# A state-space kernel with two heads: transposing loads for x, B, C, k and v, B's factor moved to C, and a shift convolution by channels

## The chip, the cores and the metric

The kernel runs on one core of a Trainium2 chip. The metric is device time in microseconds (us), the median of several timed runs; lower is better. The engines are TensorE (PE in the profile, its weight loads PEld), VectorE (DVE), ScalarE (ACT), GpSimd (POOL) and SyncE (SP), which here issues nearly all DMAs. SBUF holds one tile, the *arena*; PSUM holds one tile, *acc*, with eight banks of 512 f32 columns.

## The reference

Two heads on sequences of 2,048 steps with 640 channels, their outputs side by side in `[2048, 1280]`, inputs and output bf16:

```python
# head A: a diagonal state space with 640 complex states
dt = exp(log_dt);  Lam = Lambda_re + 1j * Lambda_im
Lam_bar = exp(dt * Lam)
B_bar = ((Lam_bar - 1.0) / Lam)[:, None] * (B_re + 1j * B_im)
Bu = einsum("bld,pd->blp", x, B_bar)
h_t = Lam_bar * h_(t-1) + Bu_t                        # 2048 steps
y = 2.0 * einsum("blp,dp->bld", h, C_re + 1j * C_im).real + x * Dskip

# head B: a short and a long convolution with gates
k_shift[s] = sum(k[s - j] * shift_k[:, j] for j in 0..3)   # zeros before the start
kv = k_shift * v
y = irfft(rfft(kv padded to 4096) * rfft(ssm_k padded to 4096))[:2048]
y = q * (y + kv * ssm_D)

out = concatenate([a, b], -1)
```

## The kernel before

**How it is ordered.** Each step is an operation of `Program.add`: a name, the engines that may do it, what it reads and writes in the arena, and a PSUM group. `depend()` derives the dependences from the footprints. The string `ORDER` (L1034), lists every operation as number, engine letter (T, V, A, G for POOL, S for SP) and first PSUM bank; `emit` issues the operations in that order, each engine's own in its order of the list, with semaphore waits for the dependences between engines. What shares a buffer or a bank waits for its last user.

**Tables.** `setup` makes the DFT tables. W (for the second transform step) is made in four chunks: an iota on POOL, two ACT operations `w_q` (L286) that multiply by the row number, a mask on DVE `w_a` (L289), and a sine on ACT (L292). G (for the last inverse step) has four chunks too: iota (L317) and integer product `g_q` (L320) on POOL, a sine on ACT (L322), two masked copies `g_k` (L325). `params` (L330) turns Lambda and dt into powers of the decay: `spread` (L420) makes 128x1280 diagonal blocks, once as GM (the factor of B) and four times as RR (the decay of the tree); DG (L427) is Dskip on diagonals; L437 to L442 make the sine and cosine of the scan's phase, the product at L440 on POOL.

**Head A.** The 640 states are ten blocks j of 64, real and imaginary part stacked on 128 partitions. B is loaded in rows (L466), and `prep_B` (L511) multiplies it by GM on TensorE (L522), which turns it at once; eviction at L528. x comes in sixteen loads of 128 rows (L474, steps of 16 in time, bit-reversed order) and is turned by TensorE in pairs (`turn_x`, L503, eviction L508). The recurrence is a tree over 16 neighbouring steps: `up2`, `up1`, `up0` (L538 to L596) take the base products B·x (`base`, L533, five of 128x512) and add the lower levels with the decay (`rmm`, L552); `coarse` (L602) scans over the 128 groups of 16 on DVE with a rotation by the phase; `down` (L638) goes back: products with the decay (L655), then either an addition on DVE (L673), or an identity product on TensorE (L653) with a copy on ACT (L671). `load_C` (L480) writes C's two planes into DRAM in the blocks' order, and one transposing DMA (L489) reads them back into the buffer that held B. `project` (L677) makes one output block of 128 rows: twenty products with C (L687, two halves of 320 columns), six with DG for x·D (L692), one copy on ACT (L696), a store (L699).

**Head B.** The long convolution of length 4,096 is a DFT in two steps of 64, in two halves (hf) of 320 channels. k is loaded with rows of 64 steps as columns (L755), its halo in small loads (L759), v alike (L768). `conv` (L780) forms the shift convolution on 2,560 elements a partition: four products with a spread table SK (`tap`, L795), three additions (L800), a product with v (L801), for each of two column sets per half; two of the 32 operations run on POOL, the rest on DVE. `s1` (L803) is the first step: ten groups of 32 products (L820) in quarters of the array, for the filter h and for k; k's stationary operands have a step of 40 elements. Evictions at L825 go to the buffer AS. `s2` (L828) is the second step: 24 products (or 16) of 160 columns in two column halves per group (L838), evicted at L851, for h into Y and for k into AS. `product` (L854) is the complex product, four times per half: pp (L862, 2,560 elements), two pq (L865), py (L867) and pz (L869), all on DVE. `r2` (L883, eviction L888) and `r1` (L904) go back; r1's eviction (L916) multiplies by q, and `store` (L928) writes. Both halves use the same AS, Y, kt, vt.

**The order of the work.** Tables, parameters and turns; up; down; in between the filter's s1 and s2 of half 0; then k's s1, the middle and the way back of half 0, half 1 alike, the sixteen projections spread over the second half and the end. `load_C` runs between up and projections.

Of the kernel before, what the change touches and what calls it, by code (L numbers as in the profile page):

```python
# [9 lines left out]
ALU = mybir.AluOpType  # L10
# [172 lines left out]
for _name, _n in (("A", 10 * 16 * 130), ("BT", 6400), ("RR", 5120), ("W", 4096), ("G", 8192), ("XT", 10240), ("AS", 10240),  # L183
                  ("Y", 10240), ("T", 7680), ("H0", 5120), ("K0", 5504), ("V0", 5120), ("YS", 2560), ("SN", 1024), ("I3", 192), ("E", 64),
                  ("JS", 128), ("F1", 128), ("IDF", 192), ("DG", 640), ("SK", 640), ("DM", 160),
                  ("PV", 70), ("SMALL", 1400)):
    LAY.part(_name, _n)


class Ctx:  # L190
    def __init__(self, nc, tc, arena, psum, ins, out):
        self.nc, self.arena = nc, arena
        self.P = Program(nc, arena, psum)
        self.ins, self.out = ins, out.rearrange("b s d -> (b s) d")
        self.CP = {nc.scalar: nc.scalar.copy, nc.vector: nc.vector.tensor_copy, nc.gpsimd: nc.gpsimd.tensor_copy}
        self.small_at = LAY.at["SMALL"][0]
# [19 lines left out]
def setup(c):  # L216
# [13 lines left out]
    P.add("js0", {V: .2}, lambda e: e.tensor_scalar_mul(out=JS[:, 0:64], in0=I3[:, 64:128], scalar1=-1.0), outs=[JS[:, 0:64]],  # L230
          ins=[I3[:, 64:128]])
    P.add("js1", {V: .2}, lambda e: e.tensor_copy(out=JS[:, 64:128], in_=I3[:, 128:192]), outs=[JS[:, 64:128]],
# [24 lines left out]
    scr = c.arena[:, LAY.at["A"][0]:LAY.at["A"][0] + 20800]  # L257
    m1 = scr[:, 20000:20064].bitcast(i32)
    q1 = scr[:, 20064:20192].bitcast(i32)
    s1 = scr[:, 20192:20320].bitcast(f32)  # L260
# [12 lines left out]
    offw = f(2)  # L273
    for lo, b, val in ((0, 0, 6144.0), (0, 1, 8192.0), (64, 0, 4096.0), (64, 1, 6144.0)):
        P.add("offw", {V: .1}, lambda e, lo=lo, b=b, val=val: e.memset(offw[lo:lo + 64, b:b + 1], val),
              outs=[offw[lo:lo + 64, b:b + 1]])
    mw = scr[:, 0:4096].bitcast(i32)
    qw = scr[:, 4096:12288].bitcast(i32)
    for ch in range(4):
        mc = mw[:, 512 * ch:512 * ch + 512]  # L280
        qc = qw[:, 1024 * ch:1024 * ch + 1024]
        q4 = qc.rearrange("p (k b c) -> p k b c", k=8, b=2)
        P.add("w_m", {G: .6}, lambda e, mc=mc, ch=ch: e.iota(mc, pattern=[[4, 8], [128, 64]], base=1 + 32 * ch,
                                                               channel_multiplier=0), outs=[mc])
        for b in range(2):
            P.add("w_q", {A: .8}, lambda e, q4=q4, mc=mc, b=b: e.activation(  # L286
                out=q4[:, :, b, :], in_=mc.rearrange("p (k c) -> p k c", k=8), func=FN.Identity, scale=p63, bias=offw[:, b:b + 1]),
                outs=[q4[:, :, b, :]], ins=[mc, p63, offw])
        P.add("w_a", {V: .7}, lambda e, qc=qc: e.tensor_single_scalar(out=qc, in_=qc, scalar=8191, op=ALU.bitwise_and),  # L289
              outs=[qc], ins=[qc])  # L290
        wo = Wt[:, 8 * ch:8 * ch + 8, :].rearrange("p k c -> p (k c)")
        P.add("w_s", {A: 1.15}, lambda e, qc=qc, wo=wo: e.activation(out=wo, in_=qc, func=FN.Sin, bias=npi, scale=SC13),  # L292
              outs=[wo], ins=[qc, npi])

    IDF = c.IDF = v("IDF")
    mi = scr[:, 20320:20448].bitcast(i32)
    qi = scr[:, 19000:19384].bitcast(i32)
# [6 lines left out]
    P.add("i_s", {A: .38}, lambda e: e.activation(out=IDF, in_=qi, func=FN.Sin, bias=npi, scale=SC13), outs=[IDF], ins=[qi, npi])  # L304

    Gt = c.G = v("G").rearrange("p (r b e a) -> p r b e a", r=2, b=64, e=2)
# [5 lines left out]
    sn = v("SN")  # L312
    for ch in range(4):
        ri, bh = ch // 2, ch % 2
# [7 lines left out]
        P.add("g_s", {A: 1.07}, lambda e, qc=qc: e.activation(out=sn, in_=qc, func=FN.Sin, scale=SC), outs=[sn], ins=[full])  # L322
        for el in range(2):
            go = Gt[:, ri, 32 * bh:32 * bh + 32, el, :]
            P.add("g_k", {V: .47, G: 2.9}, lambda e, go=go, el=el: e.tensor_scalar(  # L325
                out=go, in0=sn.rearrange("p (b a) -> p b a", a=32), scalar1=mk[:, el:el + 1], scalar2=None, op0=ALU.mult),
# [3 lines left out]
def params(c):  # L330
# [5 lines left out]
    tk = f(4)  # L336
    P.add("pr0", {V: .15}, lambda e: e.memset(pr, 0.0), outs=[pr])
    for k, src in enumerate((lam_re, lam_im, ldt_in)):
        rows = pr[10 * k:10 * k + 10, :]
        P.add("ld_par", {PSP: .1, A: .1}, lambda e, rows=rows, src=src: e.dma_start(  # L340
            out=rows.rearrange("p (a b) -> p a b", a=2), in_=bass.AP(src.tensor, 0, [[64, 10], [0, 2], [1, 64]])),
            outs=[tk[:, k:k + 1]], ins=[pr], nbytes=2560)
    rows5 = pr[30:35, :]
    P.add("ld_par", {PSP: .1, A: .1}, lambda e: e.dma_start(out=rows5, in_=dsk_in.rearrange("(a b) -> a b", b=128)),
          outs=[tk[:, 3:4]], ins=[pr], nbytes=1280)
    PV = v("PV").bitcast(f32)
    g = P.group(1)
    P.add("t_par", {PPE: .1}, lambda e, B: e.matmul(B[:, 0:35], lhsT=pr, rhs=c.I3[:, 0:35], start=True, stop=True), ins=[tk, c.I3[:, 0:35]],
          group=g, nmm=1)
    P.add("pv", {V: .25}, lambda e, B: e.tensor_copy(out=PV, in_=B[:, 0:35]), outs=[PV], group=g)  # L350
    lre, lim, ldt, dsk = PV[:, 0:10], PV[:, 10:20], PV[:, 20:30], PV[:, 30:35]
# [21 lines left out]
    for lo, mi, val in ((0, 0, 2 ** 30), (0, 1, -2 ** 31), (64, 0, 0), (64, 1, 2 ** 30)):  # L373
# [18 lines left out]
    dc, sg = f(2), f(1)  # L392
    for lo, mi, val in ((0, 0, 1.0), (0, 1, 0.0), (64, 0, 0.0), (64, 1, 1.0)):
        P.add("dc", {V: .1}, lambda e, lo=lo, mi=mi, val=val: e.memset(dc[lo:lo + 64, mi:mi + 1], val), outs=[dc[lo:lo + 64, mi:mi + 1]])
    for lo, val in ((0, 2.0), (64, -2.0)):
        P.add("sg", {V: .1}, lambda e, lo=lo, val=val: e.memset(sg[lo:lo + 64, :], val), outs=[sg[lo:lo + 64, :]])
# [56 lines left out]
class PartA:  # L453
# [57 lines left out]
    def prep_B(self, u):  # L511
# [15 lines left out]
        def ev(e, B):  # L527
            c.CP[e](out=out, in_=B[:, 0:n])  # L528
# [611 lines left out]
```

## Time and profile before

| | us |
|---|---|
| timed runs | 231.92 (median), 230.56, 231.97 |
| profiled execution | 229.08 |
| its span | 227.3 |

A busy time is the sum of an engine's instructions; idle time inside the span is a wait. How the busy times lie over the span, in stretches that follow the stages (columns: the stretch, its length, then the busy time of each engine and its instructions, TensorE's granted clock, the DMA engines' mean busy share, GB/s):

```profile
0.00:23.55 23.55, 8.79 (x83) 8.16 (x85) 19.05 (x56) 10.74 (x18) 13.60 (x31) 0.80 0.96 204
23.55:60.00 36.45, 35.02 (x498) 18.67 (x504) 31.48 (x35) 29.01 (x31) 6.56 (x5) 0.99 0.94 136
60.00:100.00 40.00, 39.09 (x618) 28.03 (x622) 31.24 (x34) 25.46 (x33) 10.98 (x5) 1.00 0.65 84
100.00:122.00 22.00, 21.70 (x248) 14.52 (x246) 20.82 (x23) 20.17 (x26) 0.76 (x1) 1.00 0.84 142
122.00:156.00 34.00, 29.05 (x883) 21.48 (x881) 32.51 (x29) 25.70 (x29) 15.54 (x4) 1.00 0.31 57
156.00:188.00 32.00, 30.81 (x631) 26.31 (x618) 20.68 (x18) 21.77 (x26) 0.00 (x0) 0.89 0.34 80
188.00:227.30 39.30, 32.57 (x623) 25.47 (x621) 25.87 (x27) 12.17 (x15) 0.00 (x0) 0.98 0.33 85
```

The order of the engines is PE, PEld, DVE, ACT, POOL. The costliest groups of the page (line, engine, operation, output and inputs, number; then the busy time and the mean of one):

```profile
L687 PE MATMUL acc<-arena 128*128 128x320 bf16 x320 | 49.9, 306 | 0.0
L533 PE MATMUL acc<-arena 128*128 128x512 bf16 x188 | 43.9, 381 | 1.7 <-issue 1.3
...
L820 PE MATMUL acc<-arena 64*64 64x64 bf16 x1280 | 28.8, 238 | 1.5 <-DVE arena L673 0.8
...
L795 DVE TENSOR_TENSOR arena<-arena 128x2560 bf16<-128x2560 bf16 x15 | 23.7, 1593 | 0.3
...
L800 DVE TENSOR_TENSOR arena<-arena 128x2560 bf16<-128x2560 bf16 x12 | 18.8, 1568 | 0.3
```

The mean of a matmul here is its time in a pipeline of several, longer than the period in which one follows another.

### The profile page before, as it was taken

The page shows a single profiled execution, that of the slowest core. Times are in us where ns is not written, and L with a number is a line of the kernel's source. Part 1 is how long each engine was busy: PE and PEld are TensorE (multiplying, and loading weights), DVE is VectorE, ACT ScalarE, POOL GpSimd, SP SyncE. Part 2 cuts the span into 40 slices and gives each one's busy share as a digit, 9 for nine tenths or more (in the row PEclk, how much of TensorE's full clock was granted, in tenths as well). Part 3 has the DMA queues.
Part 4 walks back from the last instruction along what each step waited for, and adds up shares of the span by engine and source line. Part 5 has one row for each costly group of instructions (what it writes and reads, how often), then busy time and mean ns, then how long its engine had stood idle before and what let it go on. Part 6 is the DMA issues. An engine that isn't in the chain of part 4 may idle for free.

```text
span 227.3 us, 7898 instructions
## 1 busy us (share of the span) xinstructions
PE 197.0 (87%) x3552; PEld 142.6 (63%) x3566; DVE 181.6 (80%) x217; ACT 145.0 (64%) x173; POOL 47.4 (21%) x45
## 2 busy tenths in 40 slices
PE   0715998999999999999999689997999899997793
PEld 0615544545565687786763566776888787777572
DVE  6797698969999956479999999997962489988730
ACT  2870868849669665579889779757764585148021
POOL 6592091000009400500006900074000000000000
PEclk9975899999999999999999999999979699999998
DMA  5999639999900996394992019031503700016264
GB/s 168 243 219 185 157 63 144 121 151 165 172 1 6 115 138 99 57 217 85 150 143 58 4 33 199 12 89 39 112 32 86 179 3 29 31 38 167 59 147 120
DMA packets 96782, 24.06 MB, mean 106 GB/s; under 512 B 91117, under 2 KB 96749, under 8 KB 96749
## 3 DMA queue, kind: packets, MB, share of 16 engines
q1 hardware_dynamic: 96678, 23.56, 58.7%
q8 instruction: 28, 0.46, 0.9%
q14 instruction: 6, 0.04, 0.1%
q10 hardware_dynamic: 70, 0.01, 0.0%
HBM read 16.68 MB, written 6.88 MB: 104 GB/s over the span
## 4 chain that ended last, share of the span: by engine, by line
PE 61%; DVE 25%; ACT 7%; issue 4%; DMA 1%; ACTq 0%; DVEq 0%
PE acc L687 20%; PE acc L820 10%; PE acc L838 7%; PE acc L533 7%; DVE arena L795 6%; PE acc L883 4%; DVE arena L800 4%; PE acc L692 2%; PE acc L904 2%; PE acc L503 2%; PE acc L522 2%; PE acc L552 1%; PE acc L655 1%; DVE arena L801 1%; DVE arena L420 1%
## 5 line engine op out<-in xcount | busy, mean ns | idle before, releaser
L687 PE MATMUL acc<-arena 128*128 128x320 bf16 x320 | 49.9, 306 | 0.0
L533 PE MATMUL acc<-arena 128*128 128x512 bf16 x188 | 43.9, 381 | 1.7 <-issue 1.3
L825 ACT CAST arena<-acc 128x1024 bf16<-128x1024 f32 x34 | 33.7, 1015 | 11.0 <-PE acc L820 10.9
L687 PEld LDWEIGHTS <-arena 128*128 128x128 bf16 x320 | 29.9, 100 | 12.7 <-issue 1.6
L851 ACT CAST arena<-acc 128x960 bf16<-128x960 f32 (+1 forms) x39 | 34.6, 919 | 4.9 <-PE acc L838 4.3
L696 ACT CAST arena<-acc 128x640 bf16<-128x640 f32 x16 | 11.0, 692 | 33.1 <-PE acc L692 33.1
L533 PEld LDWEIGHTS <-arena 128*128 128x128 bf16 x200 | 18.7, 99 | 20.5 <-issue 0.8
L820 PE MATMUL acc<-arena 64*64 64x64 bf16 x1280 | 28.8, 238 | 1.5 <-DVE arena L673 0.8
L820 PEld LDWEIGHTS <-arena 64*64 64x64 bf16 x1280 | 26.3, 159 | 5.9 <-issue 2.1
L838 PE MATMUL acc<-arena 128*64 128x160 bf16 x512 | 22.5, 244 | 2.1 <-ACT arena L825 1.1
L795 DVE TENSOR_TENSOR arena<-arena 128x2560 bf16<-128x2560 bf16 x15 | 23.7, 1593 | 0.3
L838 PEld LDWEIGHTS <-arena 128*64 128x64 bf16 x512 | 19.2, 115 | 5.0 <-ACT arena L825 1.6
L800 DVE TENSOR_TENSOR arena<-arena 128x2560 bf16<-128x2560 bf16 x12 | 18.8, 1568 | 0.3
L916 DVE TENSOR_TENSOR arena<-acc,arena 128x960 bf16<-128x960 f32 (+1 forms) x12 | 12.1, 1041 | 5.1 <-PE acc L904 5.0
L888 ACT CAST arena<-acc 128x1024 bf16<-128x1024 f32 x13 | 13.1, 1021 | 2.1 <-PE acc L883 1.7
L883 PE MATMUL acc<-arena 64*128 64x128 bf16 x320 | 12.1, 226 | 2.6 <-DVE arena L869 1.7
L671 ACT CAST arena<-acc 128x1024 bf16<-128x1024 f32 (+2 forms) x16 | 13.9, 933 | 0.2 <-PE acc L655 0.2
L825 DVE CAST arena<-acc 128x1024 bf16<-128x1024 f32 x6 | 7.3, 1219 | 8.3 <-ACT arena L825 6.2
L655 PE MATMUL acc<-arena 128*128 128x512 bf16 (+2 forms) x50 | 13.8, 326 | 0.0
L883 PEld LDWEIGHTS <-arena 64*128 64x128 bf16 x320 | 11.0, 145 | 4.5 <-ACT arena L671 2.2
L865 DVE TENSOR_TENSOR arena<-arena 128x1280 bf16<-128x1280 bf16 x16 | 12.8, 822 | 0.8
L862 DVE TENSOR_TENSOR arena<-arena 128x2560 bf16<-128x2560 bf16 x8 | 11.9, 1492 | 1.2 <-ACT arena L851 0.5
(134 smaller groups left out, 287.9 us busy)
## 6 DMA issues: line engine op xcount, KB each, us to landing
out_dram<-arena SPq DMA_DIRECT2D x32, 160.0 KB
arena<-in_A_x_dram SPq DMA_DIRECT2D x16, 160.0 KB
arena<-in_B_ssm_k_dram SPq DMA_DIRECT2D x8, 320.0 KB
arena<-in_B_k_dram SPq DMA_DIRECT2D x8, 320.0 KB
arena<-in_B_v_dram SPq DMA_DIRECT2D x8, 320.0 KB
arena<-in_B_q_dram SPq DMA_DIRECT2D x8, 320.0 KB
arena<-in_A_B_re_dram SPq DMA_DIRECT2D x2, 400.0 KB
arena<-in_A_B_im_dram SPq DMA_DIRECT2D x2, 400.0 KB
```

The source lines that it names most:

```text
L533: e.matmul(o, lhsT=self.BT[:, j, d, :], rhs=self.XT[:, d, t0:t0 + n], start=(d == 0), stop=(d == 4), skip_group_check=True)
L655: e.matmul(B[:, o:o + 128 * k], lhsT=c.RR[:, n, j, :], rhs=A[:, j, q:q + k, 0:128], start=not by_pe, stop=True, skip_group_check=True)
L671: e.copy(out=o, in_=b)
L687: e.matmul(B[:, 512 * b:512 * b + 320], lhsT=lh[j], rhs=self.CT[:, j, 320 * b:320 * b + 320], start=(j == 0), stop=False, skip_group_check ...
L795: P.add(f"cv{hf}m", cost, lambda e: e.tensor_tensor(out=out, in0=k, in1=bc(s, [128, 64, 40]), op=ALU.mult), outs=[out], ins=[k, c.SK[:, hf ...
L800: P.add(f"cv{hf}a", cost, lambda e, t1=t1: e.tensor_tensor(out=t1, in0=t1, in1=T2, op=ALU.add), outs=[t1], ins=[t1, T2])
L820: e.matmul(B[64 * b:64 * b + 64, 512 * l + 64 * i:512 * l + 64 * i + 64], lhsT=lh[i][ps], rhs=F[ps, b, :], start=True, stop=True, tile_pos ...
L825: P.add(f"e1{what}{hf}_{u}", {PACT: act(1024), PDVE: dve(1024)}, lambda e, B: c.CP[e](out=out, in_=B.rearrange("p (l n k s) -> p k s l n", ...
L838: e.matmul(B[64 * s:64 * s + 64, 512 * b + 160 * i:512 * b + 160 * i + 160], lhsT=c.W[:, k, 64 * b:64 * b + 64], rhs=self.AS[:, k, 160 * s ...
L851: c.CP[e](out=out, in_=b.rearrange("p r (k j n) -> p r k j n", k=n, j=4) if nj > 1 else b.rearrange("p r (k x) -> p r k x", k=n))
L883: e.matmul(B[:, 512 * s + 128 * i:512 * s + 128 * i + 128], lhsT=lh[i][s][r], rhs=rh, start=(r == 0), stop=(r == 1), tile_position=(64 * s ...
L888: P.add(f"er2{hf}_{u}", {PACT: act(1024), PDVE: dve(1024)}, lambda e, B: c.CP[e](out=out, in_=B.rearrange("p (s n b) -> p b s n", s=2, n=4 ...
```

## The change

- **B and x.** x comes in eight transposing DMAs of two row blocks each, B in four, and B's first two blocks in rows over ACT's queue, turned by TensorE. `prep_B` and `turn_x` go. Since B is no longer multiplied, real and imaginary part are two operands of 64 columns each; `base` and `rmm` issue two products in two column halves of the array in place of one.
- **B's factor.** (Lam_bar - 1)/Lam is the same for all steps, so it moves behind the recurrence, to C: two transposing DMAs load C from the inputs, and `scale_C` multiplies it by GM with 8 products in quarters of the array for each of ten pieces. GM may be spread on POOL.
- **Shift convolution by channels.** k and v come by transposing DMAs, 128 channels a chunk, time along the columns, so a tap is a shift of the address and a product with one number a partition (`cm`, L791, 14 on DVE and 6 on ACT). Three additions (L795) and the product with v (L796) on 2,048 elements: 19 on DVE, one on POOL. The result is written to DRAM (`plane`, L798) and read back in s1's layout (`relay`, L805, four loads per half), now contiguous for s1. k has one buffer, v three.
- **x times D.** `project` loads x again in rows (L705) into its output buffer, multiplies it there by a broadcast row of D (`xd`, L706, six on DVE, ten on POOL); the products with DG go, and the eviction on DVE adds (L716).
- **Buffers.** AS, Y and Z of the second half are places of their own (XT's for AS; T, KT and VT for Y).
- **Tables.** W's row number is multiplied in by one integer product on POOL a chunk (L288), whose overflow replaces the mask; G's tables are made after half 0's product stage, and `g_k` may be on ACT. Two short groups of products that only run (`warm`, L507) stand at the beginning and the end.
- **Engines and order.** Eight of the 24 steps pq, py and pz run on POOL; the order is another, with 758 operations in place of 737.

The core of the diff, without the order:

```diff
-        for b in range(2):
-            P.add("w_q", {A: .8}, lambda e, q4=q4, mc=mc, b=b: e.activation(
...
-        P.add("w_a", {V: .7}, lambda e, qc=qc: e.tensor_single_scalar(out=qc, in_=qc, scalar=8191, op=ALU.bitwise_and),
...
+        P.add("w_q", {G: 1.9}, lambda e, mc=mc, qc=qc: e.tensor_tensor(
...
+        P.add("w_s", {A: 1.015}, lambda e, qc=qc, wo=wo: e.activation(out=wo, in_=qc, func=FN.Sin, scale=SC), outs=[wo], ins=[qc])
...
+            if k == 0:
+                dst = raw[:, 640 * ri:640 * ri + 640]
+                P.add("ld_Braw", {PACT: .1}, lambda e, dst=dst, src=src: e.dma_start(out=dst, in_=src[0:128, :]), outs=[dst], nbytes=128 * 1280)
...
+            s = src[row:row + 64 * n, :].rearrange("p (d q) -> p d q", q=128)
+            P.add(f"ld_B{k}", {PSP: 64 * n * .0055}, lambda e, dst=dst, s=s: e.dma_start_transpose(out=dst, in_=s), outs=[dst],
...
+        s = self.x2.rearrange("(s r) (d q) -> r s d q", r=8, q=128)[min(ROW0[2 * g], ROW0[2 * g + 1])]
+        P.add(f"ld_x{g}", {PSP: 1.4}, lambda e: e.dma_start_transpose(out=dst, in_=s), outs=[dst], nbytes=256 * 1280)
...
+            P.add("ld_C", {PSP: 3.6}, lambda e, dst=dst, s=s: e.dma_start_transpose(out=dst, in_=s), outs=[dst], nbytes=640 * 1280)
...
+    def scale_C(self, a, h):
...
+            for r in range(2):
+                for m in range(2):
+                    for j in range(2):
+                        ps = slice(64 * j, 64 * j + 64)
+                        e.matmul(B[64 * m:64 * m + 64, 512 * j:512 * j + 320], lhsT=gm[ps, r, a, 64 * m:64 * m + 64], rhs=self.CR[ps, r, a, cs],
+                                 start=(r == 0), stop=(r == 1), skip_group_check=True, tile_position=(64 * j, 64 * m))
...
+    def base(self, e, o, j, q):
+        for d in range(5):
+            for r in range(2):
+                e.matmul(o[64 * r:64 * r + 64], lhsT=self.BT[j][:, r, d, :], rhs=self.XP[:, d, 2 * q:2 * q + 2], start=(d == 0),
+                         stop=(d == 4), skip_group_check=True, tile_position=(0, 64 * r))
...
-                for q, (d, o, n) in enumerate(pc):
-                    k0 = 64 if b and d == 2 else 0
-                    e.matmul(B[:, 512 * b + o:512 * b + o + n], lhsT=xt[d], rhs=c.DG[:, d, k0:k0 + n], start=False, stop=(q == 2),
-                             skip_group_check=True)
...
+        P.add(f"ld_r{i}", {PSP: .5}, lambda e: e.dma_start(out=ys, in_=src), outs=[ys], nbytes=128 * 1280)
+        P.add(f"xd{i}", {PDVE: dve(640, .52), PPOOL: 1.5}, lambda e: e.tensor_tensor(out=ys, in0=ys, in1=c.DR, op=ALU.mult), outs=[ys], ins=[ys, c.DR])
...
+        P.add(f"ev_C{i}", {PDVE: dve(640)}, lambda e, B: e.tensor_tensor(
+            out=ys.rearrange("p (b n) -> p b n", b=2), in0=B.rearrange("p (b n) -> p b n", b=2)[:, :, 0:320],
+            in1=ys.rearrange("p (b n) -> p b n", b=2), op=ALU.add), outs=[ys], ins=[ys], group=g)
...
+        for n, out, x in (("k", c.v("KT", 16, 2048), self.k2), ("v", c.v("VT", 2048 * (d % 3), 2048), self.v2)):
+            P.add(f"ld_{n}{d}", {PSP: 2.3}, lambda e, out=out, x=x: e.dma_start_transpose(out=out, in_=x[:, 128 * d:128 * d + 128]),
...
+        def tap(out, j):
+            k, w = c.v("KT", at - j, 2048), c.SW[:, 4 * d + j:4 * d + j + 1]
+            P.add(f"cm{d}_{j}", {PDVE: .7, PACT: act(2048)}, lambda e: c.SM[e](out, k, w), outs=[out], ins=[k, w])
+        tap(t1, 3)
+        for j in (2, 1, 0):
+            tap(t2, j)
+            P.add(f"ca{d}_{j}", tt, lambda e: e.tensor_tensor(out=t1, in0=t1, in1=t2, op=ALU.add), outs=[t1], ins=[t1, t2])
+        P.add(f"cx{d}", tt, lambda e: e.tensor_tensor(out=Vt, in0=t1, in1=Vt, op=ALU.mult), outs=[Vt], ins=[t1, Vt])
...
+            src = c.kvdram[lo:lo + 80, :].rearrange("n (a b) -> a n b", b=64)
+            P.add(f"rl{hf}_{x}", {PSP: 2.3}, lambda e, dst=dst, src=src: e.dma_start(out=dst, in_=src), outs=[dst],
+                  ins=[c.tok[:, lo // 128:(lo + 79) // 128 + 1]], nbytes=80 * 4096)
...
-            lh = [self.kv[x // 40].rearrange("p (b n) -> p b n", n=40)[:, :, x % 40] for x in gs]
+            lh = [self.KV[:, x, :] for x in gs]
...
-        n1, n2 = {PDVE: dve(2560, .52)}, {PDVE: dve(1280, .52)}
+        n1, n2 = {PDVE: dve(2560, .52)}, {PDVE: dve(1280, .52), PPOOL: 2.85}
```

419 lines of the change are left out of this document (198 added, 221 removed), and 71 rows, old and new, of the table ORDER.

## The prediction

> **What bounds the kernel now.** The first view is the page: its header, the busy times and the slices.
>
> ```profile
> span 227.3 us, 7898 instructions
> ...
> PE 197.0 (87%) x3552; PEld 142.6 (63%) x3566; DVE 181.6 (80%) x217; ACT 145.0 (64%) x173; POOL 47.4 (21%) x45
> ...
> PE   0715998999999999999999689997999899997793
> DVE  6797698969999956479999999997962489988730
> ```
>
> TensorE leads: it stands idle for 227.3 - 197.0 = 30.3 us, of which 14.8 lie before 23.55 and 3.8 behind the last product (a table of stretches); 11.7 are waits between. VectorE is the near second. The profiled execution took 229.08 us, 1.8 more than its span; the median of the timed runs, 231.92, is 1.012 times that. I sum on the span, add 1.8 and multiply by 1.012.
>
> The second view is the chain of waits, for the prices on the path. In order: the spread of B's factor; the products that wait for it; 32 products of k's first transform; 24 of k's second; 32 of the filter's first transform; two halves of projections.
>
> ```profile
> 18.16 1.50 DVE arena L420
> 19.75 3.57 PE acc L522 x32
> ...
> 99.01 1.11 PE acc L820 x32
> ...
> 105.67 0.95 PE acc L838 x24
> ...
> 137.91 0.38 PE acc L820 x32
> ...
> 189.32 1.36 PE acc L687 x10
> 190.82 1.36 PE acc L687 x10
> ```
>
> Three things to see: TensorE's first long work waits for DVE at 18 to 20 us; 32 products at L820 take 1.1 us where the stationary operand is gathered with a step of 40 elements (k) and 0.38 where it is contiguous (h); a half projection has a period of 1.50 us (190.82 - 189.32), of which 1.36 are the products with C and 0.14 those with D.
>
> The third view is the instructions in order of time between 13 and 17.5 us, POOL's and then DVE's, and SP's long issue.
>
> ```profile
> 13.11 1.89 POOL L320 TENSOR_TENSOR arena<-arena 128x1024 int32<-128x1024 int32 x1
> 14.96 2.32 POOL L440 TENSOR_TENSOR arena<-arena 128x1280 int32<-128x1280 int32 x1
> ```
>
> ```profile
> 13.16 1.94 DVE L388 TENSOR_TENSOR arena<-arena 128x80 f32<-128x80 f32 x1
> 15.14 2.18 DVE L406 TENSOR_TENSOR arena<-arena 128x20 f32<-128x20 f32 x1
> 17.35 0.18 DVE L409 TENSOR_TENSOR arena<-arena 128x20 f32<-128x20 f32 x1
> ```
>
> ```profile
> 93.47 7.61 SPq L489 DMA_TRANSPOSE arena<-c_planes  x1
> ```
>
> A DVE operation on 20 elements takes 2.18 us while a POOL product runs, and its twin 0.18 right after. The transposing transfer moves 1,638 KB between 95 and 103 us: 205 GB/s.
>
> **TensorE, term by term.** Off: the turns of x (L503, 7.0 us; ten come back for the first block of B, 10 x 110 ns = 1.1); B's preparation (L522, 4.9); k's first transform, 20 groups that now read contiguous rows, 1.08 to 0.38 each, 14.0; D's products, 32 halves x 0.14 = 4.5; the identity products that go with an addition put on ACT: of 16 such additions 4 remain in the new order, 14,464 columns become 2,944, and at 1.36 us / 3,200 = 0.425 ns a column this is 4.9. On: scaling C, 80 products of 320 columns in quarters of the array; the nearest row is L904 with quarters of 80 columns at 0.98 / 96 = 10.2 ns, four times the columns 41 ns, 3.3. The B and R products are cut in two halves of 64 columns, 300 pairs. No row has this shape; L838 is nearest, two column halves with 160 columns: 0.95 / 24 = 40 ns, 79 a pair against 68 for one alone. As a fixed 11 ns it costs 3.3 us, as a share (16% of the 55 us of L533 and L552 and kin) 9; I take 4, since pieces of 64 columns pay 20 ns too. Sum: 197.0 - 7.0 + 1.1 - 4.9 - 14.0 - 4.5 - 4.9 + 3.3 + 4 = 170.1.
>
> **VectorE.** Off: the old convolution (L795, L800, L801: 47.3); L508 3.3, L528 5.9, L289 3.4, L732 0.5, one spread 1.5, four of six g_k 3.3; eight product steps that go to POOL, 8 x 0.82 = 6.6; three evictions of L888 3.5 and 3.2 of the upward ones that go to ACT. Together 78.5. On: 19 convolution steps of 2,048, 1.49 x 0.8 = 1.2 each, 22.8; 14 taps by a scalar (ACT has six), nearest L325 with 0.47 for 1,024, so 0.94, 13.2 (0.6 to 1.3 each); the projections' evictions, now additions, 16 x 0.82 (L625) = 13.1; six x times D at 0.49, 2.9; 12 additions that were ACT's, 13.7; two evictions of C 1.6 and two of L851 2.2. Together 69.5. So 181.6 - 78.5 + 69.5 = 172.6.
>
> In these 181.6 lie DVE operations that stood beside POOL, like the pair above: row minus twin gives 1.75 + 1.7 + 2.0 + 1.5 at 2 to 17 us, 4.6 at 30 to 35, 2.8 at 70 to 77, 2.2 at 122 to 131: 16.5 us, against 39 us of POOL operations that read SBUF, a share of 0.42. DVE's own work is then 172.6 - 16.5 = 156.1. POOL's reading work grows: W's four products 9.1, G's four 9.1, the phases 4.6, the spread and r16 5.5, one convolution step 4.4, ten x times D (a quarter of L795's 5.5) 14, eight product steps at half of it 22, one g_k 3, small ones 1: 73 us. At 0.42 it takes 30.7 from DVE, whatever the eight steps saved. DVE becomes 186.8, longer than TensorE's 170.1. **That is my forecast's core: the lead passes from TensorE to VectorE.**
>
> **The way in.** B raw by ACT's queue, x and the rest of B by transposing transfers. At 205 GB/s a transfer of x (328 KB) takes 1.6 us; the second lands near 10, so up2 starts at about 10 instead of 23.6: TensorE's idle in the front falls by 5 (14.8 to 10), as little was done before. The four turns of x that ACT evicted go too; ACT gains six taps of 1.8 and four table loads of 1.28 and loses the 16 projections (11.0) and w_q (6.3): about even, beside other work. On SP each new transfer stands in one line: k's chunk d+1 waits for the taps on chunk d (one buffer), and behind it stand the filter, the last two of x and C, for which TensorE waits. The first v waits for three small tables in its buffer, done near 20. Walking it: the taps of chunk 1 end near 39, so the last x lands at 46 (needed at 49); those of chunk 2 near 50, C lands at 61 (needed at 64). The relay of half 0 ends near 80 (10.3 MB turned at 205 GB/s are 50 us, 4.5 MB plain at 204 are 22, five for landings, start at 2.5), and s1 of k could start at 79: the cover is about one microsecond. From there ACT's eight evictions at 0.97 bind, to 88; then DVE's 93 plus 0.42 x 41.5 of POOL, plus 3.8 for the last store: 202.
>
> **Forecast.** DVE 186.8, its ends 0.8 and 3.8 (the last eviction, store and landing stay), and the waits that a leading engine has now, 11: 202.4, the same as by the walk. (202.4 + 1.8) x 1.012 = **207 us**. The new wait chain at the end (store, reload of x into the same of four buffers, x times D on POOL, addition) takes some 8 us per buffer and has 9 under the last projections: nothing.
>
> **Rivals.**
> 1. TensorE stays the lead, the POOL work falling beside DVE's readings of PSUM, which the trace shows undisturbed (evictions of 1.22 and 1.23 us at 28.4 and 29.6 beside an L320 on POOL). Then 170.1 + 30.3 - 5 = 195.4, or 200 us. For it: over half of DVE's new work reads PSUM. Chance 0.27.
> 2. More than the share of now: POOL's new steps stand in the product stage, where DVE reads two SBUF operands. At 0.65, DVE is 203.6, the span 219, the time 223. Chance 0.15 for this middle ground.
> 3. **Slower: a full lock.** Each POOL step that reads SBUF stops DVE for its whole length: 156.1 + 73 + 15.6 = 244.7, 250 us. It decides from a share of (227.3 - 171.7) / 73 = 0.76 on. For: the pair above lost nearly all of both POOL operations. Against: at 149 to 156 us a POOL step of 6.3 us cost DVE nothing, its operations there reading PSUM. Chance 0.06. The Trainium skill (SBUF — State Buffer, "Who interferes with whom") states this as its rule: a VectorE instruction with two SBUF inputs and a GpSimd one that reads SBUF exclude each other for the whole instruction. By that rule offloading product steps costs more than it saves; the pair agrees with it, and the PSUM readings agree with its exception.
> 4. **Slower: the transposing transfers.** Their source steps over 1,280 or 10,240 bytes every 256, where the traced one reads whole rows. At half the rate the relay ends 50 us later, 252 span, 257 us; it decides below some 137 GB/s. Against: plain transfers of 128-byte pieces run at 215 GB/s (107 to 109 us). Chance 0.05.
> 5. The halves do not run side by side, so that the cut doubles 55 us: 170 + 51 + 25 = 246, 250 us. L838's 79 ns a pair, not 136, speaks against. Chance 0.02.
>
> The forecast has 0.42, and 0.03 goes to a time within 1% of now, by rival 2 carried further. A measurement of this kernel tells no less than about 1% from no change. Faster by more: 0.42 + 0.27 + 0.15 = 0.84; within: 0.03; slower: 0.06 + 0.05 + 0.02 = 0.13. The range leaves out the slower ones and a twentieth below rival 1, where the taps cost 0.6 and waits shrink: from 195, 5 under rival 1's 200, to 228, past rival 2's 223.
>
> **What would show it.** DVE busy near 187 and above TensorE's 170; DVE rows of one shape that split into a fast and a slow kind beside POOL; L832 at 0.4 us per 32 products; up2's first product near 10 us; the relay's transfers landing near 80. TensorE busy over 185 would say that the halves cost more; a first product of k's transform after 90, that the transfers or the single buffer hold the front; DVE below 170, that POOL takes little.

## The result and the profile after

The changed kernel took 206.96 us (median of four runs, 204.34 to 207.40) against 231.24 for the kernel before: 0.893 of it, 95% interval 0.884 to 0.902. The forecast was 207. Two later sets, with the kernel before beside them again, gave 0.916 (0.910 to 0.922; 210.08 us) and 0.906 (0.902 to 0.911; 208.18 us); the experiments below are read against the set that ran beside them where there is one, and otherwise against these three.

The time came out as forecast in the first set, the reason did not, so the match is luck. The header, busy times and slices of the changed kernel's page:

```profile
span 205.6 us, 8247 instructions
...
PE 180.7 (88%) x3713; PEld 118.7 (58%) x3713; DVE 166.2 (81%) x228; ACT 142.5 (69%) x164; POOL 76.4 (37%) x63
...
PE   2399999999999989768759999999999998999891
...
DVE  4929349798949698798697989999999899988821
...
PEclk9999999999999999999965899999999999999998
```

TensorE still has the longest busy time. It fell by 16.3 us (197.0 to 180.7) and its waits by 5.4 (30.3 to 24.9), together the 21.7 us by which the spans differ. VectorE, forecast at 186.8, has 166.2, although POOL's work did grow from 47.4 to 76.4.

The groups that answer to those shown of before (L554 is the old L533, L714 the old L687, L832 the old L820):

```profile
L554 PE MATMUL acc<-arena 128*64 128x512 bf16 x400 | 50.0, 403 | 3.9 <-issue 3.6
L714 PE MATMUL acc<-arena 128*128 128x320 bf16 x320 | 46.0, 300 | 1.4 <-DVE arena L716 0.8
...
L832 PE MATMUL acc<-arena 64*64 64x64 bf16 x1280 | 18.2, 205 | 6.9 <-ACT arena L837 3.0
...
L795 DVE TENSOR_TENSOR arena<-arena 128x2048 bf16<-128x2048 bf16 x14 | 17.8, 1268 | 5.8 <-ACT arena L198 5.5
```

The first transforms fell from 28.8 to 18.2 us, the additions of the convolution have their own place with 17.8, and L692 (D's products) is gone. The mean of L795, 1,268 ns, lies just above its undisturbed 1,220: VectorE is hardly held up by POOL there.

The middle of the chain of waits (start, length, what), as three cuts:

```profile
42.44 5.44 DMA arena<-in_B_k_dram
...
66.99 6.59 DMA arena<-in_B_k_dram
...
80.07 0.97 ACT arena L863
81.06 0.97 ACT arena L863
...
101.06 2.61 POOL arena L879
103.68 1.01 DVE arena L716
104.73 0.68 PE acc L832 x22
```

Between 42 and 74 us two transfers of k lie on the path, with ACT's and TensorE's work between them (before 42 us it is mostly TensorE's tree products), from 80 us on a row of ACT's evictions, and at 101 a single step of POOL; behind that, TensorE and VectorE are both near full until the last projections.

**Why VectorE was not slowed.** POOL's and then VectorE's instructions in order of time, where two product steps run on POOL:

```profile
117.60 2.60 POOL L881 TENSOR_TENSOR arena<-arena 128x1280 bf16<-128x1280 bf16 x1 [13.94 <-DVE arena L877]
120.28 2.61 POOL L877 TENSOR_TENSOR arena<-arena 128x1280 bf16<-128x1280 bf16 x1
```

```profile
117.77 0.82 DVE L716 TENSOR_TENSOR arena<-acc,arena 128x640 bf16<-128x640 f32 x1 [0.40 <-PE acc L714]
119.26 1.23 DVE L697 TENSOR_TENSOR arena<-acc,arena 128x1024 bf16<-128x1024 f32 x1 [0.67 <-ACT arena L863]
120.40 1.15 DVE L863 CAST arena<-acc 128x960 bf16<-128x960 f32 x1
121.46 1.22 DVE L697 TENSOR_TENSOR arena<-acc,arena 128x1024 bf16<-128x1024 f32 x1
```

Every VectorE instruction beside these two reads acc, that is PSUM, and has its ordinary length. The order does this nearly everywhere. Taken over all VectorE rows that overlap a reading POOL row, row minus undisturbed twin gives 7.2 us (1.64, 1.58 and 1.70 between 7 and 20 us, 0.64 at 23.9, 0.39 at 70.8, 0.22 at 93.8, 1.07 at 102.4, where an addition of 80 elements waits for a product step on POOL) against 66 us of such POOL work: a share of 0.11, not 0.42.

### The profile page after: what moved, and what is told of

It is laid out like the page before. It is cut to its first block, busy times and chain, and to the rows that moved or that the text cites. A ratio compares the mean times of both kernels' runs of the same rounds, so it can differ in the third digit from the quotient of the medians.

```text
span 205.6 us, 8247 instructions
## 1 busy us (share of the span) xinstructions
PE 180.7 (88%) x3713; PEld 118.7 (58%) x3713; DVE 166.2 (81%) x228; ACT 142.5 (69%) x164; POOL 76.4 (37%) x63
## 4 chain that ended last, share of the span: by engine, by line
PE 46%; ACT 24%; DVE 10%; DMA 10%; issue 5%; POOL 1%; SPq 0%; DVEq 0%; ACTq 0%
PE acc L714 14%; PE acc L554 12%; ACT arena L863 8%; ACT arena L837 7%; DMA arena<-in_B_k_dram 6%; PE acc L850 5%; PE acc L679 3%; PE acc L832 3%; PE acc L895 3%; DVE arena L716 2%; PE acc L575 2%; DVE arena L874 2%; ACT arena L198 2%; DVE arena L877 2%; PE acc L916 2%
## 5 line engine op out<-in xcount | busy, mean ns | idle before, releaser
L554 PE MATMUL acc<-arena 128*64 128x512 bf16 x400 | 50.0, 403 | 3.9 <-issue 3.6
L714 PE MATMUL acc<-arena 128*128 128x320 bf16 x320 | 46.0, 300 | 1.4 <-DVE arena L716 0.8
L554 PEld LDWEIGHTS <-arena 128*64 128x64 bf16 x400 | 23.4, 112 | 26.5 <-issue 6.5
L714 PEld LDWEIGHTS <-arena 128*128 128x128 bf16 x320 | 30.4, 98 | 14.4 <-issue 0.9
L832 PE MATMUL acc<-arena 64*64 64x64 bf16 x1280 | 18.2, 205 | 6.9 <-ACT arena L837 3.0
L706 POOL TENSOR_TENSOR arena<-arena 128x640 bf16<-128x640 bf16 x9 | 13.4, 1499 | 28.0 <-DMA arena<-in_A_x_dram 28.0
L850 PEld LDWEIGHTS <-arena 128*64 128x64 bf16 x512 | 18.2, 111 | 8.8 <-ACT arena L863 3.7
L832 PEld LDWEIGHTS <-arena 64*64 64x64 bf16 x1280 | 14.5, 117 | 14.0 <-ACT arena L837 6.2
L795 DVE TENSOR_TENSOR arena<-arena 128x2048 bf16<-128x2048 bf16 x14 | 17.8, 1268 | 5.8 <-ACT arena L198 5.5
L198 ACT ACTIVATE arena<-arena 128x2048 bf16<-128x2048 bf16 (+3 forms) x15 | 18.6, 1243 | 5.4 <-DMA arena<-in_B_k_dram 4.2
L697 DVE TENSOR_TENSOR arena<-acc,arena 128x1024 bf16<-128x1024 f32 (+2 forms) x17 | 19.2, 1148 | 1.4 <-ACT arena L863 0.7
L716 DVE TENSOR_TENSOR arena<-acc,arena 128x640 bf16<-128x640 f32 x16 | 13.3, 832 | 4.9 <-PE acc L714 4.8
L434 POOL TENSOR_TENSOR arena<-arena 128x1280 bf16<-128x1280 bf16 x1 | 2.3, 2331 | 32.1 <-ACT arena L198 32.1
L679 PE MATMUL acc<-arena 128*128 128x512 bf16 (+2 forms) x50 | 13.0, 346 | 0.6 <-ACT arena L837 0.5
L928 DVE TENSOR_TENSOR arena<-acc,arena 128x960 bf16<-128x960 f32 (+1 forms) x12 | 11.9, 1040 | 0.7 <-DMA arena<-in_B_q_dram 0.4
L874 DVE TENSOR_TENSOR arena<-arena 128x2560 bf16<-128x2560 bf16 x8 | 11.9, 1486 | 0.1
```

Source lines behind the costliest of these rows:

```text
L198: self.SM = {nc.scalar: lambda out, in_, by: nc.scalar.mul(out, in_, by), nc.vector: vm(nc.vector), nc.gpsimd: vm(nc.gpsimd)}
L554: e.matmul(o[64 * r:64 * r + 64], lhsT=self.BT[j][:, r, d, :], rhs=self.XP[:, d, 2 * q:2 * q + 2], start=(d == 0), stop=(d == 4), skip_gro ...
L679: e.matmul(B[:, o:o + 128 * k], lhsT=c.RR[:, n, j, :], rhs=A[:, j, q:q + k, 0:128], start=not by_pe, stop=True, skip_group_check=True)
L697: e.tensor_tensor(out=o, in0=b, in1=o, op=ALU.add)
L714: e.matmul(B[:, 512 * b:512 * b + 320], lhsT=lh[j], rhs=self.CT[:, j, 320 * b:320 * b + 320], start=(j == 0), stop=(j == 9))
L716: P.add(f"ev_C{i}", {PDVE: dve(640)}, lambda e, B: e.tensor_tensor(out=ys.rearrange("p (b n) -> p b n", b=2), in0=B.rearrange("p (b n) -> ...
```

## The experiments

Two theories stood against each other. *Share*, the forecast's: POOL's reading of SBUF costs VectorE 0.42 us per microsecond, and VectorE leads. *Place*: it costs VectorE only what it meets of instructions that work from SBUF, up to their full length, and nothing beside readings of PSUM; TensorE and VectorE share the lead. Then come the terms of TensorE, and the front.

### Product steps back on VectorE

```diff
 ORDER: 423, 435, 443, 457, 456, 598, 599, 633
-    "... 423G0 ... 435G0 ... 633G0 ..."
+    "... 423V0 ... 435V0 ... 633V0 ..."
```

> The eight product steps that the change put on POOL (21.5 us there) go back to VectorE, 0.82 us each; nothing else is changed. If a microsecond of POOL's reading takes 0.42 us from VectorE wherever it lies (the forecast's share), VectorE's busy time goes from 166.2 to about 166.2 + 6.6 - 9.0 = 164, and the time stays at 205 to 207. If POOL's steps cost VectorE nothing where they stand, beside its readings of PSUM, VectorE's busy time rises to about 172.5, and the time by 2 to 6 us, to 209 to 213, since VectorE is busy 4.9 of 5 us in the stretch from 120 to 170 us.

```profile
PE 179.3 (85%) x3709; PEld 118.4 (56%) x3713; DVE 172.8 (82%) x236; ACT 142.6 (68%) x164; POOL 55.4 (26%) x55
```

VectorE's busy time rose by 6.6 us, which is eight times 0.82 with nothing given back (the three profiles of the changed kernel have 166.2, 166.0 and 168.4 us, so the rise is 4.4 to 6.8, where Share says a fall of 2.4), and the time was 212.33 us (0.927, 0.921 to 0.933), 1 to 4% above the changed kernel's three ratios (the interval touches that of the highest, 0.916). Seven of the eight steps on POOL had cost VectorE nothing; only the first had met a reader of SBUF (the 1.07 us above). Share falls for these steps.

### The same POOL work in two places

```diff
+    DU, first = c.v("DU"), c.v("RR", 1280, 440)
+    c.P.add("du0", {PPOOL: .3}, lambda e: e.memset(DU, 0.0), outs=[DU])
+    for k in range(15):
+        by = DU if k else first
+        c.P.add("du", {PPOOL: 1.0}, lambda e, by=by: e.tensor_tensor(out=DU, in0=DU, in1=by, op=ALU.mult), ...)
```

> Fifteen products of 440 columns in a buffer of their own are added on POOL, some 15 us of it, from about 43 us on, where VectorE makes the shift convolution from SBUF; they do no part of the computation. If it is the place that counts (POOL's reading stops VectorE's instructions with two operands in SBUF for their length), VectorE's busy time rises by 7 to 13 us, rows of 1.22 us at the additions become 2 to 2.5 us, and the time rises by 4 to 12 us, since the relay waits for the convolution. If the share is 0.42 everywhere, VectorE gains 6 us and the time 3 to 6. If POOL takes nothing, neither moves by over 1 us.

> The same fifteen products on POOL, put between 175 and 197 us, where VectorE evicts PSUM. If the place counts, VectorE's busy time rises by less than 1.5 us (two products of x and D of 0.49 us stand there) and the time stays within 1 us of 207. If the share is 0.42 everywhere, VectorE's busy time rises by 6 us, as in the run with the convolution, and the time by 2 to 5.

The busy times, first of the run beside the convolution, then of the one beside the evictions:

```profile
PE 179.5 (85%) x3709; PEld 122.0 (58%) x3713; DVE 175.8 (83%) x228; ACT 142.7 (68%) x164; POOL 100.6 (48%) x79
```

```profile
PE 181.9 (88%) x3709; PEld 121.2 (58%) x3713; DVE 165.8 (80%) x228; ACT 142.7 (69%) x164; POOL 90.8 (44%) x79
```

Beside the evictions the fifteen products added 14.4 us to POOL (0.95 each by their rows) and nothing to VectorE (165.8), and the kernel took 207.73 us (0.904). Beside the convolution POOL's busy time rose by 24.2 us and VectorE's by 9.6; the kernel took 213.39 us (0.932, 0.925 to 0.939). By the rows, 22 us of POOL's are the fifteen products (1.5 each), and some 8 us of VectorE's lie beside them (0.5 for each); another 2 lie at 68 us, where the spread at L434, which POOL makes behind the products, met an addition. Both engines wait for each other there. VectorE's rows show it, taps and additions that are 0.75 and 1.22 us when alone:

```profile
52.06 1.21 DVE L795 TENSOR_TENSOR arena<-arena 128x2048 bf16<-128x2048 bf16 x1
53.31 1.29 DVE L197 TENSOR_SCALAR arena<-arena 128x2048 bf16<-128x2048 bf16 x1
54.64 1.83 DVE L795 TENSOR_TENSOR arena<-arena 128x2048 bf16<-128x2048 bf16 x1
56.50 1.29 DVE L197 TENSOR_SCALAR arena<-arena 128x2048 bf16<-128x2048 bf16 x1
```

Place holds, and both its ends are measured: about 0.5 us of VectorE lost for a POOL product of 0.95, or none.

### The filter of the second half loaded earlier

The scan's buffers move out of the filter's, its loads go right behind the relay, and x's rows come after them.

```diff
-        self.V = v("H0", 2560, 1280).rearrange("p (j s) -> p j s", j=10)
+        self.V = v("G", 2048, 1280).rearrange("p (j s) -> p j s", j=10)
...
-        R16 = c.v("H0", 0, 2560).bitcast(f32)
-        tA, tB = c.v("H0", 3840, 640), c.v("H0", 4480, 640)
+        R16 = c.v("T", 0, 2560).bitcast(f32)
+        tA, tB = c.v("G", 3328, 640), c.v("G", 6144, 640)
```

> The scan's buffers leave the filter's buffer (for places in G's and T's), and the second half's filter and D are loaded right behind the relay, some 8 us earlier, ahead of x's rows. In the changed kernel TensorE waits 2.4 us at 101.8 for this filter (behind an addition of 1.6 us beside a POOL step) and then runs at half clock until about 115. If that wait decides, it goes, the stretch at half clock goes with it or gets shorter, and the time falls by 2 to 6 us. If the evictions of the middle stage on ScalarE set the pace there, the waits only move, and the time stays within 1.5 us.

It took 213.80 us, against 210.08 for the changed kernel beside it (0.934 and 0.916): slower, outside both expectations. POOL's and VectorE's rows say why:

```profile
101.82 3.74 POOL L706 TENSOR_TENSOR arena<-arena 128x640 bf16<-128x640 bf16 x2 [18.13 <-DMA arena<-in_A_x_dram]
...
106.67 1.98 POOL L327 TENSOR_TENSOR arena<-arena 128x1024 int32<-128x1024 int32 x1
```

```profile
104.22 2.68 DVE L874 TENSOR_TENSOR arena<-arena 128x2560 bf16<-128x2560 bf16 x1
107.01 2.33 DVE L877 TENSOR_TENSOR arena<-arena 128x1280 bf16<-128x1280 bf16 x1
109.26 0.50 DVE L764 TENSOR_TENSOR arena<-arena 128x80 bf16<-128x80 bf16 x1
```

x's rows came later, so two POOL steps moved from 90 to 102 us and the table step from 94 to 107, onto product steps that VectorE makes from SBUF (2.68 instead of 1.49, 2.33 instead of 0.82). The scan's copy on POOL no longer waits for the filter's buffer, so it and the two table steps behind it came 8 us earlier, at 61 to 67 us, beside an addition and two taps (3.2 us). VectorE's busy time is 173.5, and TensorE still waits 2.8 us at 107, now for these. No work was added on either engine: moving loads and buffers cost VectorE 7 us. That is Place again. The half clock stayed too, from 88.7 to 98.9 and from 109.2 to 119.4 us.

### TensorE's terms: gathered k, D's products, column halves

```diff
-            lh = [self.KV[:, x, :] for x in gs]
+            lh = [self.KV.rearrange("p n b -> p (n b)").rearrange("p (b n) -> p b n", n=80)[:, :, x] for x in gs]
```

> The first transform of k takes its stationary operands with a step of 80 elements in place of contiguous ones; it reads other elements of the same buffer, so that head B's numbers are not the reference's. 20 groups of 32 products go from about 0.48 us to about 1.08: TensorE's busy time rises by 12 us, to 193. If TensorE leads, the time rises by 8 to 12 us, to 215 to 219; if VectorE led, as forecast, it would rise by less than 4.

```profile
L832 PE MATMUL acc<-arena 64*64 64x64 bf16 x1280 | 35.4, 266 | 4.9 <-ACT arena L837 1.7 <-ACT arena L863 1.2 <-issue 0.8
```

The group doubled, 18.2 to 35.4 us, TensorE's busy time went to 202.4, and the time to 225.45, 15.4 above the changed kernel beside it. That is more than expected: the twenty groups rose by 0.86 us each, from start to start, against 0.70 (1.08 less 0.38) in the kernel before. It is the step of 80 elements that does it, not the clock: the ten groups from 87 to 102 us ran at half clock (86.7 to 107 us) and took 1.27 to 1.44 us, the six from 139 to 149 us ran at full clock but for the last 0.6 us and took 1.28 to 1.41. So a step of 40, as in the kernel before, would cost less than these 15.4 us (0.70 a group for 0.86), but still a large part of what the change gained. Of 20.3 us more on TensorE (182.1 in the run beside it) three quarters show in the time.

```diff
+                for q, (o, n) in enumerate(((0, 128), (128, 128), (256, 64))):
+                    e.matmul(B[:, 512 * b + o:512 * b + o + n], lhsT=lh[q], rhs=bc(c.v("ZZ", 0, 1), [128, n]), start=False, stop=(q == 2), ...)
```

> Each projection gets its six products of 128 and 64 columns with D back, with zeros for the moving operand, while x times D stays where the change put it. The forecast priced them at 0.14 us a half, 4.5 together; the trace of before has 5.6 us between their starts and the next. TensorE's busy time rises by 4.5 to 5.6 us. Where TensorE leads (115 to 200 us, no wait over 0.8 us) all of it must show: 4 to 6 us more than the changed kernel. If VectorE led there, less than 2.

TensorE's busy time rose by 4.2 us against the run beside it (178.9 to 183.1), the time by 2.2 us (210.41 to 208.18; 0.917, 0.913 to 0.921, against 0.906). Half shows: between the two theories' numbers. With the steps on VectorE above (6.6 us of work for some 2.5 to 8 us of time) this says that from 115 us on neither engine leads alone.

```diff
-            for r in range(2):
-                e.matmul(o[64 * r:64 * r + 64], lhsT=self.BT[j][:, r, d, :], rhs=self.XP[:, d, 2 * q:2 * q + 2], start=(d == 0),
-                         stop=(d == 4), skip_group_check=True, tile_position=(0, 64 * r))
+            e.matmul(o, lhsT=self.c.v("BT", lo + 64 * n * d, 128), rhs=self.XP[:, d, 2 * q:2 * q + 2], start=(d == 0), stop=(d == 4),
+                     skip_group_check=True)
```

> The base products take one stationary operand of 128 columns in place of two of 64, and the decay's products too; the base products read other elements of B, since B's real and imaginary halves do not lie side by side, so that head A's numbers are not the reference's. 200 products of 512 columns at 216 ns (the period of the base products before) in place of 200 pairs at 241: TensorE's busy time falls by 5, from 180.7 to about 176. If TensorE sets the pace from 10 to 76 us, the time falls by 4 to 5 us, to 202 to 203. If the transfers up to the relay set it (they moved 170 to 210 GB/s from 5 to 80 us), TensorE waits that much longer and the time moves by less than 1.5 us.

```profile
L556 PE MATMUL acc<-arena 128*128 128x512 bf16 x200 | 48.8, 397 | 4.7 <-issue 3.9
```

Two hundred whole products cost 48.8 us where 200 pairs cost 50.0. Most of that difference lies in the first products, at some 427 ns each: nine here, thirteen pairs there. At full clock a pair has a period of 227 ns and a whole product 225, so the cut in halves costs about 0.4 us. The period of a whole product was 216 before; what differs is the moving operand, now four runs of 128 columns, each with a step of two elements, where it was one contiguous run of 512. Which of the two does it was not tried. The time was 209.57 us (0.912, 0.904 to 0.920), no gain.

### What sets the pace up to the relay

```diff
 ORDER: x's second load ahead of B's and of the taps; the warming products behind the turn of B
-    "... 137S0 ... 114S0 ... 127S0 ... 136S0 126S0 ..."
+    "... 137S0 136S0 127S0 126S0 114S0 ..."
```

> The second x load that the first tree products need is issued right behind the first one, ahead of two loads of B and the shift taps, and the nine warming products stand between the turn of B and the first tree product (four before it, five behind), none at the end. TensorE's first tree product then starts near 9 us in place of 10.7, and the twelve pairs that ran at 393 ns, half the clock, run at 226: 2.0 us less. If TensorE sets the pace up to the relay, the time falls by 3 to 4 us. If the transfers (k, v and the relay, which lands at 82 to 85 us) set it, TensorE gets ahead and waits longer at about 76 to 86 us, and the time moves by less than 1 us.

SP's issues of k's transfers, of the changed kernel and then of this one:

```profile
27.79 2.07 SPq L769 DMA_TRANSPOSE arena<-in_B_k_dram  x1
...
42.44 2.08 SPq L769 DMA_TRANSPOSE arena<-in_B_k_dram  x1
...
66.99 2.13 SPq L769 DMA_TRANSPOSE arena<-in_B_k_dram  x1
```

```profile
31.00 2.06 SPq L769 DMA_TRANSPOSE arena<-in_B_k_dram  x1
...
47.90 2.10 SPq L769 DMA_TRANSPOSE arena<-in_B_k_dram  x1
...
73.31 2.24 SPq L769 DMA_TRANSPOSE arena<-in_B_k_dram  x1
```

TensorE's tree began at 8.8 us in place of 10.7, at full clock, and then waited for B at 17, 21 and 25 us. The taps' load came behind, so the first chunk's taps, which free k's only buffer, came later, and every further chunk with them: 3.2, 5.5 and 6.3 us. k's first transform began at 91.5 us in place of 85.8, and the time was 212.36 us against 210.08 (0.923 and 0.916; the intervals overlap). So a delay of the first taps runs through k's one buffer and its transfers up to k's first transform, though TensorE had started earlier. How much of the time hangs on that start is not shown, since 5.7 us there gave 2.3 us at the end, within the noise. Nor is it shown that TensorE has no part in it: this run moved the taps' load as well, and the run with whole base products, which had 1.1 us less of TensorE, started k's transform at 85.2, where the changed kernel's three profiles have 85.8, 86.7 and 86.4.

### Half clock in the middle stage

TensorE ran at half clock between 104.7 and 114.9 us in the first profile of the changed kernel, at 87.7 to 98.0 and 108.2 to 115.0 in the second, at 106.7 to 113.5 in the third. The second set took 210.08 us, above what was expected of it:

> The changed kernel itself once more, as the bar for the other runs on this chip: 205 to 208 us, 0.893 of the kernel before.

> The changed kernel once more beside the two that follow: 205 to 210 us, as its two earlier runs gave. In those the record of TensorE's clock differs: half clock in the middle stage from 104.7 to 114.9 us in the one, from 87.7 to 98.0 and from 108.2 to 115.0 in the other, whose profiled execution took 2.5 us more.

```diff
         def mm(e, B):
+            if (what, hf) in (("k", 0), ("h", 1)):
+                e.matmul(B[:, 0:512], lhsT=c.I3[:, 0:128], rhs=bc(c.I3[:, 0:1], [128, 512]), start=True, stop=True)
```

> Products that compute nothing are put into TensorE's waits of the middle stage (some 80 to 115 us): one of 512 columns ahead of each group of k's first transform of half 0 and of the filter's of half 1, one of 256 ahead of each group of the second transform of half 0, and eight of 512 in the wait at 101.8 us; 8.5 us of them at full clock. If it is TensorE's low activity in this stage that brings it to half clock, the stretches at half clock between 85 and 115 us, 10.2 us and 17.1 us in the two profiles of the changed kernel, go or shrink to 3.4, TensorE's other work gets 4 to 8 us shorter, and the time falls by 2 to 5 us against the changed kernel beside it. If the half clock has another cause, it stays, and the time rises by 1 to 5 us, as the added products stand in the way.

> Of the added products only the eight of 512 columns stay (the four at the very end of the program moved ahead of the filter's first transform of half 1, and four more), in TensorE's wait of 2.37 us at about 102; at full clock they take 1.7 us and fit in it. The three profiles of the changed kernel go to half clock right behind this wait, at 104.7, 108.2 and 106.7 us, for 6.8 to 10.2 us. If the wait brings that about, the clock stays full there, TensorE's work from 104 to 115 us gets 3 to 5 us shorter, and the ratio to the kernel before falls to 0.885 to 0.90 (the changed kernel: 0.893, 0.916 and 0.906). If evictions or transfers pace that stage, the clock is full and the time within 1% of the changed kernel's.

The clock's slices, of the third profile of the changed kernel and of the kernel with fill:

```profile
PEclk9999999999999999999985999999999999999998
```

```profile
PEclk9999999999999999999999999999999999998899
```

With fill the clock stays full through the whole middle stage, so TensorE's waits there do bring the half clock about. The time went the other way and left both expectations: 216.05 us against 208.18 (0.940 and 0.906). TensorE became 12.8 us busier, 11.9 of them the added products themselves, so that its other work did not get shorter. With the eight in the wait alone the kernel took 208.25 us (0.908, 0.902 to 0.914): no difference. In the profile of that run (its longest execution, 212.87 us) the clock is at half from 96.2 to 99.6 us and full from there to 198.6: behind the filled wait it stays up. One of its executions had a mean granted clock of 1.000 and took 207.54 us, two with 0.982 took 207.26 and 207.79. So the half clock of this stage costs almost nothing; by the chain of waits above, ACT's evictions and the loads pace it, but no run tried that by itself. No version that beats the changed kernel came out of these runs.

## Why the prediction was right, and where it was wrong

**The step that failed** is this one of the sum for VectorE: "At 0.42 it takes 30.7 from DVE, whatever the eight steps saved. DVE becomes 186.8". POOL's reading work was sized well (73 us forecast, 66 measured), and so was VectorE's own work (156.1 forecast; 166.2 - 7.2 = 159.0 measured). The share was the mistake: a mean over 39 us of the old order was carried to a new order, as if it belonged to the engines. It belongs to the pairs of instructions that meet. The new order is written out in the diff: a list of what VectorE has in line where each POOL step becomes ready could have been made from it.

**Rival 1 named what happened to the busy times**, TensorE's the longest, with POOL beside readings of PSUM, at 0.27 instead of the 0.42 of the forecast. As a path TensorE alone is too much: the experiments show VectorE beside it from 115 us on, and evictions and transfers before. The rival's waits came out in sum (25.3 forecast, 24.9 measured), though not in their parts: 7.7 at the front where 9.8 was taken, 12.8 between where 11.7 was, 4.4 at the end where 3.8 was. Its TensorE work was 10.6 us too short. That is why the wrong case had the right time: 170.1 + 25.3 would have been 200 us. The terms, forecast and measured (time from each product's start to the next one's, within its own length, summed by line in both traces):

| term | forecast | measured |
|---|---|---|
| turns of x, less B's | -5.9 | -5.4 |
| preparation of B | -4.9 | -4.6 |
| k's first transform | -14.0 | -11.0 |
| D's products | -4.5 | -5.6 |
| identity products | -4.9 | -2.5 |
| scaling C | +3.3 | +3.5 |
| products in halves | +4 | +6.6 |
| warming products | not counted | +2.7 |
| sum | -26.9 | -16.3 |

- *k's first transform*: all forty groups took 0.43 us on the mean, not 0.38, some of them at half clock. The direction and most of the size were right, and it is by far the largest term.
- *Halves*: about 0.4 us is the cut, as the whole products show, less than the 4 that were taken. The rest is not the cut: the moving operand's new layout (9 ns x 200 = 1.8), thirteen slow pairs at the start (5.4 us in place of 2.9: 2.5; the record of the clock begins at 16.0 us, where the pairs become fast, so half clock is inferred from their period), and twelve products that the old trace does not record (188 of 200 rows, 12 x 0.216 = 2.6); against these stand two old products at half clock (0.4).
- *Identity*: the products that remain got longer (L655's 8.9 us against L679's 10.9). More of them now stand right ahead of a product of another shape, where up to 0.33 us pass to the next start in place of 0.22.
- *Warming products*: eight of 512 columns, 2.7 us of busy time, were in the diff and left out of the sum. Half of them lie in a wait at the front, half behind the last projection.

**The front**: up2 began at 10.7 (forecast about 10), and the transfers, between 5 and 25 us nearly all transposing ones, moved 171 to 189 GB/s there and 138 to 215 in stretches of 5 us up to 80 us (205 taken; rival 4, below 137, is refuted). k's transform could start at 85.8, not 79. The "cover of about one microsecond" did not exist: the relay's start hangs on the chain over k's one buffer, as the run with x's load moved shows.

**The other rivals**: 2 and 3 are refuted as stages of this kernel, by the share of 0.11, but the lock of rival 3 is real where two readers of SBUF meet (about 0.5 us for a product of 0.95). The POOL step that rival 3 names as harmless (149 to 156 us) had met one such reader: a product of the convolution (L795) at 149.36, started just before it, took its ordinary 1.49 us, and POOL's step took 6.3. The page "SBUF — State Buffer" of the Trainium skill ("Who interferes with whom") says that a VectorE instruction with at most one SBUF input, outside the two-port modes, does not contend with GpSimd; the evictions above agree, at 0.82 and 1.15 to 1.23 us. It counts tensor_scalar among the operations that may enter a two-port mode and contend; the taps agree, at 1.29 us beside POOL and 0.75 alone. Rival 5 is refuted: 227 ns a pair, not 432.

## What to carry to other kernels

A price for two engines' contention belongs to the pair of instructions that overlap, not to the engines: before summing it, list for each step on POOL what VectorE has in line there, and put it beside readings of PSUM. Work on POOL that is placed so cost nothing here, and a load moved by ten microseconds can undo the place. Where a sum of busy times meets the time, check each engine's sum by itself: here an engine forecast 20.6 us too long and another 10.6 too short met at the right total.

## What had not been expected of the hardware

- TensorE goes to half clock without any long idle time: in the changed kernel's middle stage the longest wait before these stretches is 2.4 us, and in one profile 1.0 us (85.6 us, half clock from 87.7); in the 3.4 us before them TensorE was busy for 27 to 52%. The stretches last 6.8 and 10.2 us, two and three times 3.4. The Trainium skill (TensorE: Matmul & The Clock Gate, "What's actually happening") states a free-running window of 3.4 us and idle windows as the cause; the lengths agree with the window, while here windows that are partly busy suffice. Products with a gathered stationary operand can do it without any wait: half clock begins at 167.7 us in the kernel before, behind 4 us of them alone, and at 134.5 and 148.2 in the run with k gathered, and in the 3.4 us before each of the three the profile has TensorE busy all the time. Why stays open.
- A moving operand in four runs of 128 columns with a step of two elements costs 225 ns for 512 columns, against 216 in one contiguous run.
- A stationary operand with a step costs much more: 32 products of 64 columns took about 0.4 us contiguous, 0.95 to 1.15 with a step of 40 elements and 1.28 to 1.41 with one of 80.
- Blocking between VectorE and POOL hits both: a POOL product of 0.95 us takes 1.5 beside the convolution.
